# Attention scores: the last halving and the sum over four partitions done by TensorE into the softmax layout

## The chip, the core and the metric

The kernel runs on one core of one Trainium2 chip. The metric is the device time of one execution in microseconds (us). Engines are named as in the profile: PE is TensorE (matrix products; PEld its weight loads), DVE is VectorE, ACT is ScalarE, POOL is GpSimd, SP is SyncE, which issues most transfers. Each engine works through its own queue in order; an instruction that has to wait holds up everything behind it on that engine.

## What is computed

The input x has 2048 rows of 1024 in bf16. After a layer norm without weights it goes through two branches, and the output is x + s * g:

```
xn = layernorm(x)
qkv = xn @ wqkv            # 32 heads of 32; q, k, v
logits[h, s, w] = (q[h, s] . k[h, s - 2w]) * 32**-0.5,  w = 0..7   (-1e9 where s - 2w < 0)
s  = (softmax(logits, over w) . v[h, s - 2w]) @ wo
g  = silu( (silu(xn @ w1) * (xn @ w3)) @ w2 )          # w1, w3: 1024 x 3584, w2: 3584 x 1024
out = x + s * g
```

So each position attends to eight positions, two apart, in its own head.

## The kernel before

The rows are worked in two blocks (b) of 1024, each of two chunks (c) of 512 positions. Layer norm and a transpose on PE (`ln_tp`) give xT, features on partitions. `qkv(c)` makes q, k and v of a chunk with 3 x 8 groups of 8 matmuls; each group fills one of the eight PSUM banks, and ACT casts it to SBUF (L220): q into `qo`, k into `kT`, v into `vT`. `kT` and `vT` hold one chunk and a halo of 16 older positions, which POOL copies from the chunk before (L201, L202) ahead of the new casts. The MLP's products (`mlp_up` in 14 parts `fb`, `mlp_down`) are done with a Strassen-like scheme that trades matmuls for additions on DVE and copies on ACT. One part of `mlp_up` has the groups ua, ue, ub; its last group (with `a22` and `t4`, "the tail") is put off into the next part through `pend`, and `flush` emits it. `wo(c)` multiplies the attention's result by wo and DVE (L541, L542) applies gate and residual.

The feature dimension of q and k is laid out so that partition p of slice j holds feature 8p + j of the 1024, so a head's 32 features lie in 4 neighbouring partitions of all 8 slices. `attention(c)` therefore works in these steps:

- Scores, for each of the 8 offsets w: DVE multiplies q by the shifted kT in two halves of four slices (L236, 128x2048 each), adds the halves (L238), halves again (L239) and once more (L240) into `E[:, w]`. What is left is a sum over 4 neighbouring partitions.
- Softmax layout: 16 transfers issued by POOL (L244) take every fourth partition of E into two tiles L, so that a partition is a head and a quarter of the positions; three DVE adds (L248 to L250) sum the four partitions into z, in fp32.
- Softmax on z: for chunk 0 a mask (L252), max tree, subtraction (L255), exp on ACT (L256), sum tree, reciprocal (L260), product into `pb` (L261). 16 transfers on POOL (L264) spread pb back over E, each value to the four partitions of its head.
- PV: DVE multiplies E by the shifted vT (L272) and adds up (L280, L286, L287) into `qo`.

`E` has one buffer. Intermediate tiles of the attention (`p_t`, `L`, `z`, `zm`, `zs`, `pb`, `B`, `C`) share a pool of three. A scheduling layer orders each engine's instructions when the program is built: by priority in the order in which the code emits them, filling in lower ones where it expects an engine to be free; `tc.high_priority()` moves instructions ahead. The emitted order is:

```
    for b in range(NB):
        qkv(c0); ...; mlp_up(b, range(cut[b])); attention(c0); flush(); qkv(c1)
        mlp_up(b, range(cut[b], FB)); flush(); attention(c1); mlp_down(b); wo(c0)
    wo(3)
```

with cut = (11, 10), FB = 14, and the wo of a block's second chunk behind the next block's first qkv. In block 0, DVE also makes sums of the weights in each part (`w_sums`, `w2_sums`, four adds each). At the start of `mlp_down`, DVE makes sums of h (L463, L464, L478, L490).

Of the kernel before, what the change touches and what calls it, by code (L numbers as in the profile page):

```python
# [9 lines left out]
BF16 = mybir.dt.bfloat16  # L10
FP16 = mybir.dt.float16
ACTF = mybir.ActivationFunctionType
ALU = mybir.AluOpType
# [4 lines left out]
def kernel(  # L18
# [21 lines left out]
    nc = tc.nc  # L40
    P = 128
    S, D, F = 2048, 1024, 3584
    Dh, W, DIL = 32, 8, 2
    KT = D // P
    KH = KT // 2
    CH = 512
# [6 lines left out]
    HALO = 16  # L53
    NJ = 8
    NR = 4
# [12 lines left out]
    const = ctx.enter_context(tc.tile_pool(name="const", bufs=1))  # L68
# [5 lines left out]
    att = ctx.enter_context(tc.tile_pool(name="att", bufs=3))  # L74
# [12 lines left out]
        out=ident[:], in_=ident[:], compare_op=ALU.not_equal, fill=1.0,  # L87
        base=0, pattern=[[-1, P]], channel_multiplier=1,
# [3 lines left out]
    nc.gpsimd.affine_select(  # L92
        out=maskb[0:32], in_=maskb[0:32], compare_op=ALU.is_ge, fill=-1.0e9,
        base=0, pattern=[[-DIL, W], [1, HALO]], channel_multiplier=0,
    )

    kT = keep.tile([P, NJ, HALO + CH], BF16, name="kT")
# [5 lines left out]
    E = keep.tile([P, W, CH], BF16, name="E")  # L103
# [21 lines left out]
    def bank(name):  # L125
        return psum.tile([P, CH], FP32, tag="mm", name=name)
# [97 lines left out]
    def tree(t, z, op):  # L224
        op(t[:], z[:, 0:4, :], z[:, 4:8, :])
        op(t[:, 0:2, :], t[:, 0:2, :], t[:, 2:4, :])
        op(t[:, 0:1, :], t[:, 0:1, :], t[:, 1:2, :])

    def attention(c):
        qT = qo[:, c % 2]  # L230
        for w in range(W):
            o = HALO - DIL * w
            pr = []
            for jh in range(2):
                p_t = att.tile([P, 4, CH], BF16, tag="a4")
                nc.vector.tensor_mul(p_t[:], qT[:, jh * 4:jh * 4 + 4, :], kT[:, jh * 4:jh * 4 + 4, o:o + CH])  # L236
                pr.append(p_t)
            nc.vector.tensor_add(pr[0][:], pr[0][:], pr[1][:])  # L238
            nc.vector.tensor_add(pr[0][:, 0:2, :], pr[0][:, 0:2, :], pr[0][:, 2:4, :])  # L239
            nc.vector.tensor_add(E[:, w, :], pr[0][:, 0, :], pr[0][:, 1, :])  # L240
        L = [att.tile([P, 2, W, P], BF16, tag="a4", name=f"L{c}_{i}") for i in range(2)]
        for r in range(NR):
            for sq in range(4):
                nc.gpsimd.dma_start(  # L244
                    out=L[r // 2][sq * 32:(sq + 1) * 32, r % 2, :, :], in_=E[r:P:NR, :, sq * P:(sq + 1) * P],
                )
        z = att.tile([P, W, P], FP32, tag="a4", name=f"z{c}")
        nc.vector.tensor_add(z[:], L[0][:, 0], L[0][:, 1])  # L248
        nc.vector.tensor_add(z[:], z[:], L[1][:, 0])
        nc.vector.tensor_add(z[:], z[:], L[1][:, 1])  # L250
        if c == 0:
            nc.vector.tensor_add(z[:, :, 0:HALO], z[:, :, 0:HALO], maskb[:])  # L252
        zm = att.tile([P, W // 2, P], FP32, tag="a4", name=f"zm{c}")
        tree(zm, z, nc.vector.tensor_max)
        nc.vector.tensor_sub(z[:], z[:], zm[:, 0:1, :].to_broadcast([P, W, P]))  # L255
        nc.scalar.activation(out=z[:], in_=z[:], func=ACTF.Exp, scale=scale)  # L256
        zs = att.tile([P, W // 2, P], FP32, tag="a4", name=f"zs{c}")
        tree(zs, z, nc.vector.tensor_add)
        pb = att.tile([P, W, P], BF16, tag="a4", name=f"pb{c}")
        nc.vector.reciprocal(out=zs[:, 0, :], in_=zs[:, 0, :])  # L260
        nc.vector.tensor_mul(pb[:], z[:], zs[:, 0:1, :].to_broadcast([P, W, P]))  # L261
        for r in range(NR):
            for sq in range(4):
                nc.gpsimd.dma_start(  # L264
                    out=E[r:P:NR, :, sq * P:(sq + 1) * P], in_=pb[sq * 32:(sq + 1) * 32, :, :],
                )
        for jh in range(2):
            js = slice(jh * 4, jh * 4 + 4)

            def pvmul(dst, w):  # L270
                o = HALO - DIL * w
                nc.vector.tensor_mul(  # L272
                    dst, E[:, w, :].unsqueeze(1).to_broadcast([P, 4, CH]), vT[:, js, o:o + CH]
                )

            A = qT[:, js, :]
            pvmul(A, 0)
            B = att.tile([P, 4, CH], BF16, tag="a4")
            pvmul(B[:], 1)
            nc.vector.tensor_add(A, A, B[:])  # L280
            for w0 in (2, 4, 6):
                B = att.tile([P, 4, CH], BF16, tag="a4")
                C = att.tile([P, 4, CH], BF16, tag="a4")
                pvmul(B[:], w0)
                pvmul(C[:], w0 + 1)
                nc.vector.tensor_add(B[:], B[:], C[:])  # L286
                nc.vector.tensor_add(A, A, B[:])  # L287
# [259 lines left out]
    for b in range(NB):  # L547
        c0, c1 = 2 * b, 2 * b + 1
        qkv(c0, partial(ln_transpose, 1) if b == 0 else None)
        if b == 0:  # L550
            w2_load(0)
        else:
            wo(c0 - 1)
        xn_sums()
        mlp_up(b, range(cut[b]))
        attention(c0)
        flush()
        qkv(c1)
        mlp_up(b, range(cut[b], FB))
        flush()  # L560
        attention(c1)
        mlp_down(b)
        wo(c0)
# [31 lines left out]
```

## Time and profile before

| | us |
|---|---|
| time, median of 2 runs (768.35 and 770.64) | 769.5 |
| span of the profiled execution, first to last instruction | 766.9 |
| PE busy, 3516 matmuls | 749.4 |
| DVE busy, 828 instructions | 602.1 |
| ACT busy, 534 instructions | 321.1 |
| POOL busy, 172 instructions | 97.2 |
| score multiplies L236, 64 of 1.215 | 77.5 |
| last halving L240, 32 of 0.414 | 13.3 |
| transfers E to L, L244, 64 issues of 0.586 | 37.0 |
| additions of L, L248 to L250, 12 of 1.217 | 14.6 |
| transfers pb to E, L264, 64 issues of 0.582 | 36.8 |

The busy time of a group is the sum of its durations, in which neighbouring instructions can overlap: matmuls with 512 columns last 0.379 us each and follow each other faster than that. A row of the order in time has the start, the length, engine, line, operation, what it writes and reads, how many instructions are merged, and in brackets the engine's idle time just before with what ended it. The page's chain follows the work that ended last back from the last instruction.

### The profile page before, as it was taken

How to read it: one execution, taken by the hardware profiler on the slowest of the kernel's cores; microseconds unless marked ns; L12 is line 12 of the kernel's file. 1: busy time of each engine (PE TensorE's matmuls, PEld its weight loads, DVE VectorE, ACT ScalarE, POOL GpSimd, SP SyncE). 2: the span in 40 equal slices, each digit the busy share in tenths (PEclk: the TensorE clock that was granted, in tenths of full speed). 3: DMA queues.
4: the chain of work that ended last, by engine and by line, in shares of the span. 5: the costliest groups of instructions: out<-in, count | busy, mean ns of one | idle time of the engine just before them, and what ended most of it. 6: DMA issues, size and time to landing. Idle time of an engine off the chain costs nothing.

```text
span 766.9 us, 9404 instructions
## 1 busy us (share of the span) xinstructions
PE 749.4 (98%) x3516; PEld 375.6 (49%) x3516; DVE 602.1 (79%) x828; ACT 321.1 (42%) x534; POOL 97.2 (13%) x172
## 2 busy tenths in 40 slices
PE   7999999999899999999999899999999999999997
PEld 4664444444565444445566344444466544444443
DVE  6479988887998999150799998565995995924997
ACT  5536444654225489264033044464433444321200
POOL 0000042132000001413000004040000004040000
PEclk8999999999999999999999999999999999999999
DMA  9633799898753668658853836565535257464634
GB/s 331 217 111 108 234 302 272 275 285 297 261 189 83 218 227 268 172 190 262 261 179 103 270 114 169 175 195 165 187 115 201 98 172 207 157 196 147 200 100 140
DMA packets 123117, 150.56 MB, mean 196 GB/s; under 512 B 6080, under 2 KB 97728, under 8 KB 119488
## 3 DMA queue, kind: packets, MB, share of 16 engines
q1 hardware_dynamic: 110336, 115.36, 48.2%
q0 software_dynamic: 8128, 30.42, 11.7%
q10 hardware_dynamic: 4608, 4.20, 1.6%
q8 instruction: 27, 0.44, 0.3%
q14 instruction: 18, 0.15, 0.1%
HBM read 115.34 MB, written 26.21 MB: 185 GB/s over the span
## 4 chain that ended last, share of the span: by engine, by line
PE 86%; DVE 8%; DMA 4%; issue 1%; ACT 1%; SPq 0%; DVEq 0%; ACTq 0%
PE ub L120 18%; PE qkv L120 15%; PE ue L120 12%; PE ua L120 12%; PE db L120 9%; PE de L120 6%; PE da L120 6%; PE s L120 5%; DMA wt<-in_A_wqkv_dram 2%; DVE B L286 1%; DVE B L272 1%; DVE qo L287 1%; DVE p_t L236 1%; PE tp L182 1%; DVE C L272 1%
## 5 line engine op out<-in xcount | busy, mean ns | idle before, releaser
L120 PE MATMUL qkv<-xT,wt 128*128 128x512 bf16 x768 | 169.9, 383 | 4.9 <-DMA wt<-in_A_wqkv_dram 4.4
L120 PEld LDWEIGHTS <-wt 128*128 128x128 bf16 x768 | 110.1, 144 | 63.8 <-DMA wt<-in_A_wqkv_dram 5.8
L120 PEld LDWEIGHTS <-st 128*128 128x128 f16 x896 | 87.7, 98 | 107.4 <-issue 1.7
L120 PE MATMUL ua<-xT,w 128*128 128x512 bf16 x448 | 106.7, 381 | 2.9 <-ACT ub L131 2.9
L120 PEld LDWEIGHTS <-w 128*128 128x128 bf16 x672 | 65.9, 98 | 84.0 <-issue 5.9
L120 PE MATMUL ub<-xs,st 128*128 128x512 f16 x448 | 106.7, 381 | 0.0
L120 PEld LDWEIGHTS <-h_sb 128*128 128x128 bf16 (+1 forms) x672 | 65.5, 98 | 77.5 <-issue 0.5
L236 DVE TENSOR_TENSOR p_t<-qo,kT 128x2048 bf16<-128x2048 bf16 x64 | 77.5, 1215 | 8.5 <-ACT kT L220 8.5
L120 PE MATMUL db<-wt,h_sb 128*128 128x512 f16 x336 | 73.7, 379 | 0.0
L374 DVE TENSOR_TENSOR us<-ue,us 128x512 f32<-128x512 f32 x56 | 37.5, 685 | 38.3 <-PE ue L120 38.3
L120 PE MATMUL s<-wot,qo 128*128 128x512 bf16 x256 | 55.7, 379 | 0.0
L367 ACT ACTIVATE h_sb<-ua 128x512 bf16<-128x512 f32 x56 | 33.3, 598 | 53.3 <-PE ua L120 53.3
L385 ACT ACTIVATE sg<-us 128x512 bf16<-128x512 f32 x56 | 34.8, 630 | 46.7 <-DVE us L374 46.7
L120 PE MATMUL ub<-xs,w 128*128 128x512 f16 x224 | 53.4, 379 | 0.9 <-DVE h_sb L383 0.9
L120 PE MATMUL ue<-xs,st 128*128 128x512 f16 x224 | 52.9, 379 | 0.1
L120 PE MATMUL ue<-xT,st 128*128 128x512 bf16 x224 | 52.9, 379 | 0.0
L131 ACT COPY ub<-ua 128x512 f32<-128x512 f32 x56 | 31.6, 570 | 44.4 <-PE ua L120 25.4
L120 PE MATMUL da<-wt,h_sb 128*128 128x512 bf16 x224 | 49.2, 379 | 0.3 <-DMA wt<-in_B_w_dram 0.3
L264 POOL DMA_DIRECT2D E<-pb x64 | 36.8, 582 | 92.9 <-DVE pb L261 89.1
L397 DVE TENSOR_TENSOR h_sb<-h_sb,ub 128x512 bf16<-128x512 bf16 x56 | 37.0, 679 | 14.4 <-PE ub L120 14.4
L244 POOL DMA_DIRECT2D L<-E x64 | 37.0, 586 | 59.3 <-DVE E L240 55.6
L220 ACT CAST qo<-qkv 128x512 bf16<-128x512 f32 x32 | 18.6, 585 | 61.3 <-PE qkv L120 45.0
(103 smaller groups left out, 841.1 us busy)
## 6 DMA issues: line engine op xcount, KB each, us to landing
wt<-in_A_wqkv_dram SPq DMA_DIRECT2D x24, 1024.0 KB, 7.1
w<-in_B_w_dram SPq DMA_DIRECT2D x42, 512.0 KB, 5.1
s_dram<-st POOLq DMA_DIRECT2D x14, 1024.0 KB, 5.9
wt<-t_dram SPq DMA_DIRECT2D x16, 896.0 KB, 5.4
st<-s_dram SPq DMA_DIRECT2D x14, 1024.0 KB, 5.3
wt<-in_B_w_dram SPq DMA_DIRECT2D x12, 896.0 KB, 6.1
wot<-in_A_wo_dram SPq DMA_DIRECT2D x8, 1024.0 KB, 7.9
w2q<-in_B_w_dram SPq DMA_DIRECT2D x14, 512.0 KB, 3.8
```

The lines of the kernel that those rows point to most:

```text
L120: nc.tensor.matmul(ps[:], lhsT=lhs[k], rhs=rhs[k], start=(first and k == 0), stop=(k == n - 1), skip_group_check=not first,)
L131: nc.scalar.copy(out=dst[:], in_=src[:])
L182: nc.tensor.matmul(tp[:, k * P:(k + 1) * P], lhsT=xt4[:, st, kt * P:(kt + 1) * P], rhs=ident[:], start=(k == 0), stop=(k == KH - 1), skip_ ...
L220: nc.scalar.copy(out=dst, in_=ps[:])
L236: nc.vector.tensor_mul(p_t[:], qT[:, jh * 4:jh * 4 + 4, :], kT[:, jh * 4:jh * 4 + 4, o:o + CH])
L244: nc.gpsimd.dma_start(out=L[r // 2][sq * 32:(sq + 1) * 32, r % 2, :, :], in_=E[r:P:NR, :, sq * P:(sq + 1) * P],)
L264: nc.gpsimd.dma_start(out=E[r:P:NR, :, sq * P:(sq + 1) * P], in_=pb[sq * 32:(sq + 1) * 32, :, :],)
L272: nc.vector.tensor_mul(dst, E[:, w, :].unsqueeze(1).to_broadcast([P, 4, CH]), vT[:, js, o:o + CH])
L367: nc.scalar.activation(out=h_sb[:, fl[i], 0:CH], in_=pa[i][:], func=ACTF.Silu)
L374: m = nc.vector.tensor_add(su2[i][:], pe[i][:], su2[i][:])
L385: nc.scalar.activation(out=sg2[i][:], in_=su2[i][:], func=ACTF.Silu)
L397: nc.vector.tensor_mul(h_sb[:, fl[i], 0:CH], h_sb[:, fl[i], 0:CH], pb[i][:])
```

## The change

The last halving and the sum over four partitions are done by PE. `bones` is a 128x32 matrix of ones and zeros with bones[p, h] = 1 where p // 4 = h, built once by POOL. E now holds, for four offsets at a time, the two slices that are left after L239's halving (`E4`, 4 offsets x 2 slices x 512 positions). For each half of the offsets, eight matmuls with `bones` as the weights sum over the four partitions and the two slices, and write heads and quarters of positions straight into the layout of z in one PSUM bank, `zb`; ACT copies the bank into z.

```diff
+    bones = const.tile([P, 32], BF16, name="bones")
+    nc.gpsimd.memset(bones[:], 1.0)
+    nc.gpsimd.affine_select(
+        out=bones[:], in_=bones[:], compare_op=ALU.is_ge, fill=0.0,
+        base=0, pattern=[[-NR, 32]], channel_multiplier=1,
+    )
+    nc.gpsimd.affine_select(
+        out=bones[:], in_=bones[:], compare_op=ALU.is_ge, fill=0.0,
+        base=NR - 1, pattern=[[NR, 32]], channel_multiplier=-1,
+    )
...
     def attention(c):
         qT = qo[:, c % 2]
-        for w in range(W):
-            o = HALO - DIL * w
-            pr = []
-            for jh in range(2):
-                p_t = att.tile([P, 4, CH], BF16, tag="a4")
-                nc.vector.tensor_mul(p_t[:], qT[:, jh * 4:jh * 4 + 4, :], kT[:, jh * 4:jh * 4 + 4, o:o + CH])
-                pr.append(p_t)
-            nc.vector.tensor_add(pr[0][:], pr[0][:], pr[1][:])
-            nc.vector.tensor_add(pr[0][:, 0:2, :], pr[0][:, 0:2, :], pr[0][:, 2:4, :])
-            nc.vector.tensor_add(E[:, w, :], pr[0][:, 0, :], pr[0][:, 1, :])
-        L = [att.tile([P, 2, W, P], BF16, tag="a4", name=f"L{c}_{i}") for i in range(2)]
-        for r in range(NR):
-            for sq in range(4):
-                nc.gpsimd.dma_start(
-                    out=L[r // 2][sq * 32:(sq + 1) * 32, r % 2, :, :], in_=E[r:P:NR, :, sq * P:(sq + 1) * P],
-                )
+        E4 = E[:].rearrange("p (w j) t -> p w j t", j=2)
         z = att.tile([P, W, P], FP32, tag="a4", name=f"z{c}")
-        nc.vector.tensor_add(z[:], L[0][:, 0], L[0][:, 1])
-        nc.vector.tensor_add(z[:], z[:], L[1][:, 0])
-        nc.vector.tensor_add(z[:], z[:], L[1][:, 1])
+        for wh in range(2):
+            for w4 in range(4):
+                o = HALO - DIL * (wh * 4 + w4)
+                pr = []
+                for jh in range(2):
+                    p_t = att.tile([P, 4, CH], BF16, tag="a4")
+                    nc.vector.tensor_mul(p_t[:], qT[:, jh * 4:jh * 4 + 4, :], kT[:, jh * 4:jh * 4 + 4, o:o + CH])
+                    pr.append(p_t)
+                nc.vector.tensor_add(pr[0][:], pr[0][:], pr[1][:])
+                nc.vector.tensor_add(E4[:, w4], pr[0][:, 0:2, :], pr[0][:, 2:4, :])
+            zb = bank(f"zb{c}_{wh}")
+            for jj in range(2):
+                for sq in range(4):
+                    nc.tensor.matmul(
+                        zb[sq * 32:(sq + 1) * 32, :], lhsT=bones[:], rhs=E4[:, :, jj, sq * P:(sq + 1) * P],
+                        start=(jj == 0), stop=(jj == 1), skip_group_check=True,
+                    )
+            with tc.high_priority():
+                nc.scalar.copy(out=z[:, wh * 4:wh * 4 + 4, :], in_=zb[:].rearrange("p (w t) -> p w t", w=4))
```

Below, line numbers of the kernel before are used for instructions that both kernels have.

## The prediction

> **What bounds the kernel now.** I read the page's busy shares and chain first, then who waited for whom on TensorE (PE), then the order in time of PE, VectorE (DVE) and GpSimd (POOL) around the four attention calls. Busy shares, then the chain's shares by engine:
>
> ```profile
> PE 749.4 (98%) x3516; PEld 375.6 (49%) x3516; DVE 602.1 (79%) x828; ACT 321.1 (42%) x534; POOL 97.2 (13%) x172
> ...
> PE 86%; DVE 8%; DMA 4%; issue 1%; ACT 1%; SPq 0%; DVEq 0%; ACTq 0%
> ```
>
> PE is the bound; DVE is idle for 165 us of the span. PE's own waits (us in total, times, longest):
>
> ```profile
> PE qkv L120 <- DMA wt<-in_A_wqkv_dram: 4.4, 3, 3.5
> PE ua L120 <- ACT ub L131: 2.9, 1, 2.9
> PE ub L120 <- DVE h_sb L383: 0.9, 3, 0.4
> ```
>
> No row has PE waiting for attention: scores, softmax and PV run on DVE, POOL and ScalarE (ACT) beside the MLP's matmuls. PE in order of time (start, length, work, idle before):
>
> ```profile
> 186.85 1.89 PE L120 MATMUL ub<-xs,st 128*128 128x512 f16 x8
> 189.07 1.89 PE L120 MATMUL ub<-xs,w 128*128 128x512 f16 x8 [0.33 <-DVE h_sb L383]
> 194.50 5.79 PE L120 MATMUL qkv<-xT,wt 128*128 128x512 bf16 x18 [3.55 <-DMA wt<-in_A_wqkv_dram]
> ...
> 350.92 0.83 PE L182 MATMUL tp<-ident,x 128*128 128x128 bf16 x12
> 351.59 0.38 PE L120 MATMUL db<-wt,h_sb 128*128 128x512 f16 x1
> ...
> 379.00 41.60 PE L120 MATMUL qkv<-xT,wt 128*128 128x512 bf16 x192
> ...
> 440.79 2.76 PE L120 MATMUL ua<-xT,w 128*128 128x512 bf16 x8 [2.92 <-ACT ub L131]
> 443.34 2.75 PE L120 MATMUL ub<-xs,st 128*128 128x512 f16 x8
> 445.93 1.89 PE L120 MATMUL ue<-xT,st 128*128 128x512 bf16 x8
> ```
>
> Start to start, a 512-column matmul takes 41.6/192 = 0.216 us and a 128-column one (351.59 - 350.92)/12 = 0.056. After an idle of 2.9 us the next two groups of 8 take 2.55 and 2.59 us where others take 1.73: a restart costs 1.7 us, and the granted clock there is 0.71. DVE in order of time, then POOL:
>
> ```profile
> 194.91 1.22 DVE L272 TENSOR_TENSOR qo<-E,vT 128x2048 bf16<-128x2048 bf16 x1
> ...
> 225.94 1.22 DVE L272 TENSOR_TENSOR C<-E,vT 128x2048 bf16<-128x2048 bf16 x1
> ...
> 230.70 2.35 DVE L236 TENSOR_TENSOR p_t<-qo,kT 128x2048 bf16<-128x2048 bf16 x2
> 232.97 1.22 DVE L238 TENSOR_TENSOR p_t<-p_t 128x2048 bf16<-128x2048 bf16 x1
> 234.22 0.69 DVE L239 TENSOR_TENSOR p_t<-p_t 128x1024 bf16<-128x1024 bf16 x1
> 234.83 1.22 DVE L236 TENSOR_TENSOR p_t<-qo,kT 128x2048 bf16<-128x2048 bf16 x1
> ...
> 673.71 1.23 DVE L261 TENSOR_TENSOR pb<-z,zs 128x1024 bf16<-128x1024 f32 x1
> ...
> 692.13 1.23 DVE L272 TENSOR_TENSOR qo<-E,vT 128x2048 bf16<-128x2048 bf16 x1 [16.19 <-DMA E<-pb]
> ```
>
> ```profile
> 227.32 1.12 POOL L202 COPY vT<-vT 128x128 bf16<-128x128 bf16 x1 [31.48 <-DVE C L272]
> ...
> 342.08 9.15 POOL L264 DMA_DIRECT2D E<-pb x16 [26.82 <-DVE pb L261]
> ```
>
> **Removed.** Per chunk: 8 adds of L240 (0.34 us start to start), 3 z additions (1.14) and 16 L transfers (9.3 us of POOL issue). All of it lies beside PE: worth 0 on the path, 24 us of DVE in sum. It could pay only where PE waits for a late DVE. That is the 2.92 us at 440.79: the forks (L131) waited 18.9 us in all for DVE's o_t of L541 to free banks, and DVE was late there with chunk 1's PV. With PV done earlier (below) I take that wait and its restart away: -4.6 (ends 0 and -4.6).
>
> **Moved onto PE's queue.** The changed kernel's instructions stand thus. Scores are made in two halves of four offsets. zb's first 8 matmuls stand just before the last s4 group ("tail") of the MLP part ahead of the attention, the second 8 right behind it (chunks 1 and 3: 1 ahead of the last tail group, 15 behind), and all qkv or `da` matmuls behind those. DVE cannot begin the second half's E before the first 8 matmuls have read E, which has one buffer. So PE now waits at the second 8 until DVE has made a half. A half: two multiplies 2.27 us, add 1.25, E add 0.61, and 0.12 where the add follows its own multiply (as 1.25 against 1.14 above): 4.25 per offset, 17.0 in all. From the tail's end to E ready:
>
> - Chunk 0: DVE has the last L397 (0.8 with the signal), two w_sums (1.2), four w2_sums (1.34) and the half, 16.8 as its first steps are interleaved: 20.1. The weights' wait of 3.55 and two later ones (0.84) fall inside: 20.1 - 3.55 - 0.84 = +15.7. The restart was paid before.
> - Chunk 1: L397 0.8, eight L463/L464 at 1.0, one w2_sum and small steps 1.3, the half 17.0: 27.1; restart 1.7; two small waits (0.4) gone: +28.4.
> - Chunk 2: 0.8 and the half less one multiply already done, 15.8: 16.6; restart 1.7, an old 0.41 gone: +17.9.
> - Chunk 3: half of the L463/L464 lie ahead of the tail's end: 0.8 + 0.6 + 4.0 + 3.2 + 17.0 = 25.6; restart 1.7: +27.3.
>
> **What is late next.** In chunks 0 and 2 everything from the softmax to PV now starts with qkv of the next chunk, where it was over or begun before. From the end of zb: copy 0.8, mask 0.3 (chunk 0), max and subtract 2.7, table and exp 2.4, sums to pb 3.7, transfers, PV to its last C 32.25 (194.91 to 227.16), vT's halo copy 1.3, first vT cast 0.8. For the transfers there are two rows: pb's end 674.94 to 692.13 is 17.2; 9.15 of issue and the page's median landing of 4.6 give 14.1 after pb; I take the middle, 15.6. Sum 59.9 (chunk 2: 59.6). PE has 192 matmuls ahead of it, 41.6 + 1.7 = 43.3, and then needs a PSUM bank that holds v, as all 8 do. It waits 16.6 and 16.3 more, with a second restart each: +18.3 and +18.0. In chunks 1 and 3 the same chain has `mlp_down` (89 us, 276 to 365) as cover: 0; without it up to 60.
>
> **Added.** 64 matmuls with 512 columns moving and 32 output columns. 14 lie inside the waits; 50 count. No row has 32-column weights. By moving columns 0.216 each, 10.8; a quarter of the array writes as much as a 128-column matmul, so 0.056, 2.8. They are as near to one row as to the other: middle, 6.8, both ends kept. The 8 z copies on ACT (0.57, as L131) are in the chain above; `bones` costs POOL three short steps at the start, 0.8 by the rows of `ident` and `maskb` (0.2 + 0.3 + 0.3), with 185 us until its first use.
>
> The Trainium skill bears on this price. "TensorE: Matmul & The Clock Gate", Part 3 (packing small matmuls), says matmuls that write different 32-row slices of PSUM run at once; an estimate by it is a quarter of 10.8, and the time would be 4 us below mine. Against the change, "TensorEngine Tiling (Array Packing)", Key Properties, says a change of tiling mode drains TensorE; with 0.38 - 0.22 = 0.16 us left after the last start and 16 changes, an estimate is +2.6. No run here shows either.
>
> **Sum.** 15.7 + 28.4 + 17.9 + 27.3 = 89.3 first waits; 18.3 + 18.0 = 36.3 second waits; 6.8 matmuls; -4.6. Together +127.8 on the profiled execution's span of 766.9: 894.7. The median 769.5 lies 2.6 above that span, for the work around it: **897 us**.
>
> **Rivals.**
> 1. DVE runs ahead and E is ready when PE comes: no first waits, then PV as early as before. For it: DVE's 165 idle us, 24 more freed. Against it: the second half's writes wait for zb's first half, which stands 1.7 us ahead of the second. It decides if that order lets DVE start 17 us sooner. Then +6.8 - 4.6: 772, not slower. Chance 0.03.
> 2. The second waits are hidden: qkv's v banks are cast late but nothing needs them. It decides if PV ends within 43 us of zb, a chain shorter by 17. For it: in the trace vT's halo copy held ACT up only by 6.9 us in all. Against: the terms are rows, and the 32.25 of PV alone leaves 11. 897 - 36 = 861. Chance 0.09.
> 3. DVE backlog: after the second wait DVE owes chunk 1's (3's) first half beside the MLP. Three (four) MLP parts at 12.1 us of PE and some 8 to 9 us of DVE leave 3 to 4 each; if nothing of it is left, up to 17 us show in each: 897 + 34 = 931. Against: at 246 to 275 DVE had as much and PE waited 0.2. Chance 0.09.
> 4. The four matmuls that write the four partition slices of zb run at once: 50 x 0.216/4 = 2.7, so 893. No row shows two matmuls at once; chance 0.35, inside the forecast's own range. (The Trainium skill's rule above says it would be so.)
>
> That the change doesn't do what it says I leave out: the instructions named as removed are gone from the queues.
>
> **Numbers.** Forecast 0.44 and rival 4 0.35 share a range: zb 2.8 to 10.8 and 2.6 of drains (-4 to +6.6), transfers 14.1 to 17.2 twice (-3 to +3.2), the 4.6 not gained (+4.6): 890 to 912. Out to rivals 2 and 3: 861 to 931; each of these has a spread of its own, so that about 0.15 with rival 1 is left out. Faster by over 2% 0.01, within 2% 0.02, slower by over 2% 0.97; 2% is about what a measurement of this kernel tells from no change.
>
> **What would show it.** Four waits of PE in `zb` rows on DVE E, 17 to 27 us long, just behind the last `ub` tails; two waits of `ua` on ACT vT of about 17 us behind qkv of chunks 1 and 3; the granted clock near 0.7 behind each; no wait of `ua` near wo(1). PE's busy time up by 3 to 11 us, DVE's down by 24 to 28. Wrong would be: E written before the tail; vT cast on time; zb groups of 8 taking far from 0.45 to 1.7 us at full clock; waits of PE inside the MLP.

## The result and the profile after

| | before | after |
|---|---|---|
| time, median of 2 runs, us | 769.5 | 898.6 |
| span of the profiled execution | 766.9 | 896.2 |
| PE busy | 749.4 | 762.2 |
| PE not busy (span less busy) | 17.5 | 134.0 |

The kernel after is slower: the ratio is 1.166, with a 95% interval of 1.156 to 1.175. Forecast were 897 us and a rise of 127.8 in the span; the span rose by 129.3. Of this, 116.5 is time in which PE stands and 12.8 is time in which it works. From here on, lines of the kernel after and of the experiments are lines of those kernels: in the kernel after, L250 to L253 are the scores, L257 is zb, L284 PV and L231 the casts of q, k and v.

Busy shares and the chain's shares by engine, on the page of the kernel after:

```profile
PE 762.2 (85%) x3519; PEld 377.8 (42%) x3580; DVE 590.7 (66%) x784; ACT 322.1 (36%) x539; POOL 60.9 (7%) x111
...
PE 72%; DVE 21%; POOL 2%; DMA 2%; issue 2%; ACT 1%; SPq 0%; DVEq 0%; POOLq 0%; ACTq 0%
```

DVE has less to do than before (590.7 for 602.1 us), yet its share of the chain has gone from 8% to 21%: it is not busier, PE now stands for it. The rows of PE's waits (us in total, times, longest) say where:

```profile
PE zb L257 <- DVE E L253: 89.2, 4, 26.5
PE ua L131 <- ACT vT L231: 30.5, 2, 16.0
PE qkv L131 <- DMA wt<-in_A_wqkv_dram: 1.3, 2, 1.0
...
PE ua L131 <- ACT ub L142: 0.7, 1, 0.7
```

The first two rows are new and come to 119.7; the others were 4.4 and 2.9. PE in order of time shows where each wait stands and what follows it:

```profile
189.06 0.61 PE L257 MATMUL zb<-E,bones 128*32 128x512 bf16 x8
189.60 1.90 PE L131 MATMUL ub<-xs,w 128*128 128x512 f16 x8
211.83 1.05 PE L257 MATMUL zb<-E,bones 128*32 128x512 bf16 x8 [20.33 <-DVE E L253]
212.81 20.55 PE L131 MATMUL qkv<-xT,wt 128*128 128x512 bf16 x81
...
273.10 3.21 PE L131 MATMUL ua<-xT,w 128*128 128x512 bf16 x8 [14.47 <-ACT vT L231]
...
338.39 1.05 PE L257 MATMUL zb<-E,bones 128*32 128x512 bf16 x8 [26.50 <-DVE E L253]
...
639.55 1.04 PE L257 MATMUL zb<-E,bones 128*32 128x512 bf16 x8 [17.22 <-DVE E L253]
...
700.12 3.57 PE L131 MATMUL ua<-xT,w 128*128 128x512 bf16 x8 [16.04 <-ACT vT L231]
...
777.62 1.04 PE L257 MATMUL zb<-E,bones 128*32 128x512 bf16 x8 [25.11 <-DVE E L253]
```

Each chunk has one wait at the second zb group, behind the first and the 1.9 us of the tail; chunks 0 and 2 have a second wait one qkv later. A zb group itself takes 0.54 us from its start to the next one's, and 0.98 behind a wait.

### The profile page after: what moved, and what is told of

Same layout as the page of the kernel before. It is cut to its first block, busy times and chain, and to the rows that moved or that the text cites. A ratio compares the mean times of both kernels' runs of the same rounds, so it can differ in the third digit from the quotient of the medians.

```text
span 896.2 us, 9343 instructions
## 1 busy us (share of the span) xinstructions
PE 762.2 (85%) x3519; PEld 377.8 (42%) x3580; DVE 590.7 (66%) x784; ACT 322.1 (36%) x539; POOL 60.9 (7%) x111
## 4 chain that ended last, share of the span: by engine, by line
PE 72%; DVE 21%; POOL 2%; DMA 2%; issue 2%; ACT 1%; SPq 0%; DVEq 0%; POOLq 0%; ACTq 0%
PE ub L131 15%; PE ua L131 11%; PE ue L131 11%; PE qkv L131 10%; PE db L131 8%; PE s L131 6%; PE da L131 6%; DVE p_t L250 4%; PE de L131 4%; DVE B L284 2%; DVE p_t L252 2%; POOL E L276 2%; DVE C L284 2%; DVE qo L299 2%; DVE B L298 2%
## 5 line engine op out<-in xcount | busy, mean ns | idle before, releaser
L131 PE MATMUL qkv<-xT,wt 128*128 128x512 bf16 x751 | 172.1, 389 | 3.0 <-DMA wt<-in_A_wqkv_dram 1.3
L131 PE MATMUL ua<-xT,w 128*128 128x512 bf16 x441 | 108.5, 387 | 31.6 <-ACT vT L231 30.5
L250 DVE TENSOR_TENSOR p_t<-qo,kT 128x2048 bf16<-128x2048 bf16 x64 | 76.2, 1217 | 20.8 <-ACT kT L231 20.8
L257 PE MATMUL zb<-E,bones 128*32 128x512 bf16 x64 | 7.4, 502 | 89.2 <-DVE E L253 89.2
L409 DVE TENSOR_TENSOR h_sb<-h_sb,ub 128x512 bf16<-128x512 bf16 x56 | 37.1, 682 | 32.9 <-PE ub L131 32.9
L131 PE MATMUL da<-wt,h_sb 128*128 128x512 bf16 x218 | 51.5, 396 | 0.7 <-issue 0.4
L553 DVE TENSOR_TENSOR o_t<-s,xs 128x512 f32<-128x512 f32 x32 | 21.9, 688 | 35.3 <-PE s L131 35.3
```

Source lines behind the costliest of these rows:

```text
L131: nc.tensor.matmul(ps[:], lhsT=lhs[k], rhs=rhs[k], start=(first and k == 0), stop=(k == n - 1), skip_group_check=not first,)
L409: nc.vector.tensor_mul(h_sb[:, fl[i], 0:CH], h_sb[:, fl[i], 0:CH], pb[i][:])
L553: nc.vector.tensor_mul(o_t[:], ps[:], gt[:, dh * NST + st])
```

## The experiments

Four theories were tried. **T**, the forecast's: the time goes into PE standing in its queue for a half of the scores that is late, and after that for late PV. **M**: it goes into the zb matmuls themselves, some 16 us per group. **D**: DVE has too little time for the scores, whatever the order. And within T, what makes the half late: only E (**Te**), or E and a place in a pool (**Tp**). The kernels below were measured in three groups of four, each beside the kernel before, whose medians there were 770.4 (own_E, early, late, both), 771.8 (touch_z, own_E_touch_z, early_pv, both_pv) and 770.3 (warm, sq_outer, zb_x4, own_all). As these and the 769.5 above differ by up to 2.3, a difference of 2 us between kernels of two groups means little.

### own_E: E is not shared

Each offset has its own place in E, at the price of the third halving on DVE:

```diff
-                nc.vector.tensor_add(E4[:, w4], pr[0][:, 0:2, :], pr[0][:, 2:4, :])
+                nc.vector.tensor_add(pr[0][:, 0:2, :], pr[0][:, 0:2, :], pr[0][:, 2:4, :])
+                nc.vector.tensor_add(E[:, wh * 4 + w4, :], pr[0][:, 0, :], pr[0][:, 1, :])
...
-            for jj in range(2):
-                for sq in range(4):
+            for sq in range(4):
...
-                        zb[sq * 32:(sq + 1) * 32, :], lhsT=bones[:], rhs=E4[:, :, jj, sq * P:(sq + 1) * P],
-                        start=(jj == 0), stop=(jj == 1), skip_group_check=True,
+                    zb[sq * 32:(sq + 1) * 32, :], lhsT=bones[:], rhs=E[:, wh * 4:wh * 4 + 4, sq * P:(sq + 1) * P],
+                    start=True, stop=True, skip_group_check=True,
...
```

> The third halving is kept on DVE, so each offset has its own place in E, the second half of the scores no longer waits for the first zb group, and a zb group has 4 matmuls. Theory T (the loss is PE standing in its queue at the second zb group for a half of the scores that could not begin before the first group had read E, and after that late PV): the waits of zb on DVE vanish in chunks 0, 2 and 3, where DVE had time ahead of the tail (it was free of scores from 722 to 752 in chunk 3), the wqkv weights' wait of 3.5 comes back, chunk 1 still waits 25 to 29, since DVE was busy 37.8 of 39 us ahead of it, and both vT waits stay at 13 to 16: 898.6 - 16.4 - 16.8 - 25 - three restarts of 2.5 + 2 for the adds = about 835 (828 to 845). Rival M (the zb matmuls or their mode cost the time, some 16 us per group of 8): half the matmuls, so about 834 too, but with PE's time in matmuls and not in waits. Rival D (DVE has too little time for the scores, whatever the order): waits stay within 3 us of what they were, 890 to 905.

Measured: 902.7 us, ratio 1.172 (1.169 to 1.175). The theory missed by 68. Not one wait has gone; its row of PE's waits:

```profile
PE zb L256 <- DVE E L253: 97.1, 4, 28.4
```

DVE of the same run, in order of time around chunk 0:

```profile
61.16 0.42 DVE L253 TENSOR_TENSOR E<-p_t 128x512 bf16<-128x512 bf16 x1
65.11 0.69 DVE L385 TENSOR_TENSOR us<-ue,us 128x512 f32<-128x512 f32 x1 [3.53 <-PE ue L131]
...
193.25 1.22 DVE L249 TENSOR_TENSOR p_t<-qo,kT 128x2048 bf16<-128x2048 bf16 x1
```

The fourth offset is done at 61.6. DVE then stands for 3.5 us for PE and makes no scores until 193, though q, k and E are there: the products of the fifth offset are not waiting for anything, they stand far behind in DVE's queue. The kernel after shows the same in chunk 3, where DVE had little else to do:

```profile
722.38 0.69 DVE L253 TENSOR_TENSOR E<-p_t 128x1024 bf16<-128x1024 bf16 x1
...
760.40 2.35 DVE L250 TENSOR_TENSOR p_t<-qo,kT 128x2048 bf16<-128x2048 bf16 x2
```

The products write `p_t`, not E, so E cannot be what kept them. M is half refuted as well: half the matmuls in as many groups, the same time. D fits the number, and so does a second hold.

### touch_z and own_E_touch_z: the place in the pool

What the products need is a buffer of the pool of three, and in the code `z` stands ahead of them but is written for the first time when ACT copies the first zb group. If z holds the place of the second half's buffers until then, an earlier write to z frees them. The edit is one line, on the kernel after and on own_E:

```diff
         z = att.tile([P, W, P], FP32, tag="a4", name=f"z{c}")
+        nc.gpsimd.memset(z[:, 0, 0:1], 0.0)
```

> The kernel after, and POOL writes one column of z ahead of the scores of each chunk, so that z takes its place in the pool of three (a4) before the scores do and not at its first copy from zb; E is still shared by both halves. Theory Tp (two things hold the second half: its first products need p_t buffers, which come behind z in the pool, and z is taken only when the first zb group has run; and its sums need E): DVE can make one pair of products and their sum ahead, 3.5 us, and no more, so the four zb waits fall by 2.5 to 3.5 each (89.2 to about 77) and the time is about 886 (880 to 892). Theory Te (only E holds it): no change, 896 to 901. Rival D (DVE has too little time): no change.

> own_E with the same early write of z, so that neither E nor the pool holds the second half. Tp: the zb waits of chunks 0 and 2 vanish and the weights' wait of 3.5 comes back; chunk 3 keeps 8 to 10 (the sums of h and the last offset behind the tail); chunk 1 keeps 25 to 29, as DVE is busy in the three parts ahead of it; both vT waits stay at 13 to 16, since softmax and PV still begin with the next qkv: 898.6 - 16.3 - 16.8 - 16 - restarts 5 = about 845 (835 to 855). Te and D: as own_E, 898 to 906.

| | E shared | E not shared |
|---|---|---|
| z first written by the copy | 898.6 (after) | 902.7 (own_E) |
| z written early | 880.9 (touch_z) | 852.8 (own_E_touch_z) |

touch_z: ratio 1.143 (1.140 to 1.147); the four zb waits are 15.5, 24.6, 12.4 and 20.4, 73.0 in all for 89.2. Three of them fell by 4.7 to 4.8 and not by 3.5, as DVE also makes one product of the next pair. own_E_touch_z: ratio 1.107 (1.103 to 1.111), with these waits:

```profile
PE zb L257 <- DVE E L254: 39.6, 3, 28.4
PE ua L131 <- ACT vT L231: 33.1, 2, 16.7
PE qkv L131 <- DMA wt<-in_A_wqkv_dram: 4.5, 3, 3.1
PE ua L131 <- ACT ub L142: 3.0, 1, 3.0
```

So there are two holds in series. Freeing E alone gains nothing, freeing the pool alone 17.7, both 45.9. With both free the waits of chunks 0 and 2 are gone or nearly so (39.6 is 28.4 of chunk 1, 10.9 of chunk 3 and 0.3), the weights' wait of 3.1 is back, and the vT waits are as they were. That one early write frees the products shows that z's place is the second hold; how the building hands out the places is not to be seen in a trace. Te falls and D falls, but for chunk 1: there DVE was busy 37.8 of the 39 us ahead of the tail in the kernel after, and the 28.4 stays.

### early and early_pv: the first chunk's attention stands earlier

`attention` is taken apart into scores and zb of one half, softmax (`soft`) and PV (`pv`), which are emitted behind parts of `mlp_up`. In `early`, PV goes along with the softmax; in `early_pv` it stays behind the last part:

```diff
-        mlp_up(b, range(cut[b]))
-        attention(c0)
+        mlp_up(b, range(cut[b]), {1: [partial(scores, c0, 0)], 5: [partial(scores, c0, 1), partial(soft, c0)]})
+        pv(c0)
```

> For the first chunk of each block the first zb group stands behind part 1 of the MLP and the second, with softmax and PV, behind part 5, in place of part 10 (9); the second chunk of each block stands as it did. Theory T: both waits of chunks 0 and 2 vanish, zb on DVE (20.3 and 17.2) and ua on vT (14.5 and 16.0), with their restarts (some 8 in all); the weights' waits of 4 to 5 come back; chunks 1 and 3 still wait 25 to 28: 898.6 - 68 + 5 - 8 = about 827 (820 to 836). M: 64 matmuls as before, so 895 to 902. D: the waits return inside the MLP parts or in chunks 1 and 3, 850 or more.

Measured: 859.9, ratio 1.117 (1.114 to 1.119). The two vT waits and the zb waits of chunks 0 and 2 are gone, and 51.6 of zb is left for chunks 1 and 3, as expected. But there is a new wait of 31.3, and the time is 33 above the 827 expected; by the time alone it lies in D's range (850 or more). PE's rows:

```profile
PE zb L261 <- DVE E L257: 51.6, 2, 26.5
PE ue L131 <- DVE st L354: 31.8, 2, 31.3
```

DVE at the end of that wait:

```profile
212.34 1.22 DVE L306 TENSOR_TENSOR B<-B,C 128x2048 bf16<-128x2048 bf16 x1
213.47 0.68 DVE L354 TENSOR_TENSOR st<-w 128x1024 f16<-128x1024 bf16 x1
214.07 1.22 DVE L307 TENSOR_TENSOR qo<-qo,B 128x2048 bf16<-128x2048 bf16 x1
```

The weight sums (`st`) of the next part have PV's B and qo rows directly ahead of them: PV, emitted earlier, had come before them in DVE's queue. This is the same fault as in the change itself, made by the experiment: the engine that bounds stands for work put ahead of what it needs.

> As the run early (zb of the first chunk of each block behind parts 1 and 5, softmax behind part 5), but PV emitted at its old place behind part 10 (9), so that it does not stand ahead of the next part's weight sums on DVE, for which PE stood 31.3 us in early. Theory T (PE loses time only where it stands for DVE in its queue): the waits of chunks 0 and 2 vanish, chunks 1 and 3 keep 26.5 and 25.1: 859.9 - 31.3 - 2 to 3 for the restart = about 826 (820 to 832). Rival: the DVE work only moves, and another wait of 10 or more appears in the MLP: 836 to 860.

Measured: 832.3, ratio 1.080 (1.077 to 1.084), just above the theory's range: the 31.3 is gone, no other long wait has come in the MLP, and the weights' waits are 8.3 where the expectation of `early` had 4 to 5. So the wait in `early` was PV's place in the queue, and not DVE having too little time (D).

### late, both, both_pv and own_all: the second chunk too

The second zb group, softmax and PV of the second chunk of each block stand inside `mlp_down` (in `late` and `both` behind the T2 products; in `both_pv` so in block 0, and behind the first gate products in block 1). The cut is that of `both_pv`; in the other two, softmax and PV are one function:

```diff
-        attention(c1)
-        mlp_down(b)
+        scores(c1, 0)
+        mlp_down(b, (partial(scores, c1, 1), partial(soft, c1), partial(pv, c1)))
```

> For the second chunk of each block the second zb group, softmax and PV stand 36 us further on, behind the T2 products of mlp_down; the first chunk of each block stands as it did. Theory T: the zb waits of chunks 1 and 3 (26.5 and 25.1) and their restarts (about 2 each) vanish, the four waits of chunks 0 and 2 stay: 898.6 - 51.6 - 4.5 = about 842 (836 to 852, the upper end if PV is late for wo(3)). M: 895 to 902. D: 870 or more.

> Both moves together, with all 64 zb matmuls. Theory T: no wait on scores or vT is left, the sum of the two gains: 898.6 - 71 - 56 = about 771 (766 to 780), the time before plus 3 to 4 us of zb matmuls on PE and with the weights' waits back, and the wait at the first ua of block 1 gone or back (-4.6 or 0). M: 895 to 902. D: 800 or more, with waits of zb or of ua on DVE in the MLP.

> early_pv, and in the second chunk of each block the second zb group, softmax and PV stand inside mlp_down: behind the T2 products in block 0 (36 us on), behind the first gate products in block 1 (24 us on, since PV was 10.0 us late for the last wo in the run both). Theory T: no wait on scores is left but up to 5 us of zb in block 1: 771 to 780, within 2% of the time before (770.4), though all 64 zb matmuls are done. M (the matmuls themselves cost): 820 or more.

`late` took 856.3 (ratio 1.112, 1.110 to 1.115): the zb waits of chunks 1 and 3 are gone (37.5 is left, chunks 0 and 2), and the last `wo` stands 10.0 us for PV, so it is 4 above the range. `both` took 820.7 (1.066, 1.063 to 1.069), far over the 780 expected and by the time alone in D's range (800 or more); its long waits are the 31.3 of `early` and the 10.0 of `late`, and none is on scores. `both_pv` took 788.2 (1.023, 1.019 to 1.027), 8 above the range; its waits:

```profile
PE qkv L131 <- DMA wt<-in_A_wqkv_dram: 6.8, 4, 4.6
PE s L131 <- DVE qo L310: 6.3, 1, 6.3
...
PE zb L261 <- DVE E L257: 1.1, 1, 1.1
```

All 64 zb matmuls are there, and of the 129 us some 16 are left: M is refuted. What is left is mostly PV late for the last `wo` and weights that come later, not scores.

The last of this line, `own_all`, keeps the third halving on DVE, emits all scores ahead of z, and has both zb groups together where E is sure to be ready:

```diff
+    def zsum(c):
+        zt[c] = att.tile([P, W, P], FP32, tag="a4", name=f"z{c}")
...
+        mlp_up(b, range(cut[b]), {1: [partial(scores, c0, 0), partial(scores, c0, 1)], 6: [partial(zsum, c0), partial(soft, c0)]})
+        pv(c0)
...
+        mlp_down(b, (partial(zsum, c1), partial(soft, c1), partial(pv, c1)))
```

> The third halving is kept on DVE, E holds all eight offsets, all scores are emitted ahead of z, and both zb groups (4 matmuls each) stand where E is sure to be ready: behind part 6 in the first chunk of each block, 36 us into mlp_down in block 0, 12 us into it in block 1; softmax behind them, PV of the first chunks at its old place. Theory: nothing of the loss is left but the matmuls, and the wait of wo for PV (6.3 in both_pv) goes as PV of the last chunk starts 12 us earlier: 788.2 - 6.3 - 2 - 2 = about 778 (773 to 784), still not under the time before (771), since PE is the bound and has 32 matmuls more. Rival: DVE, which has the third halving back, is late in block 0 or 1: 784 to 800.

Measured: 784.1, ratio 1.017 (1.014 to 1.020): at the edge of the theory's range and in that of the rival, and both are partly right. No wait for scores or PV is left, but

```profile
PE qkv L131 <- DMA wt<-in_A_wqkv_dram: 9.6, 4, 5.3
PE ub L131 <- DVE h_sb L414: 3.3, 4, 1.7
PE ue L131 <- DVE st L360: 2.9, 1, 2.9
PE ua L131 <- ACT ub L142: 2.4, 1, 2.4
```

come to 18.2, where the kernel before had 8.2 in the three rows that the prediction shows. PE is busy for 751.7 us, 2.3 more than before. So the change can be had for about 14 us in place of 129. `own_all` is within 2% of the kernel before, but its interval lies above 1, and so do those of all the others; no version tried beats the kernel before: PE had no wait on the scores there that could be saved.

### warm: does PE's standing slow what follows?

On the kernel after; the extra matmuls write into the bank that zb then overwrites:

```diff
             zb = bank(f"zb{c}_{wh}")
+            if wh == 1:
+                flush()
+                for i in range((90, 118, 75, 111)[c]):
+                    m = nc.tensor.matmul(zb[:], lhsT=ident[:], rhs=kT[:, 0, 0:CH], start=True, stop=True, skip_group_check=True)
...
```

> The kernel after, and PE is given 90, 118, 75 and 111 matmuls of 128 columns of weights and 512 moving columns between the last tail group and the second zb group of chunks 0 to 3, work that fits just inside the waits there (19.4, 25.5, 16.2 and 24.0 of 20.3, 26.5, 17.2 and 25.1 us); their result is overwritten by the zb group. The waits of ua on vT are not filled. If what follows a long wait is slow because the clock granted to PE has sunk (0.50 for some 4 us and 0.64 to 0.88 for 4 more in the kernel after), the granted clock stays at 1.00 there and 2 to 3 us per chunk are saved, 898.6 - 9.5 = about 889 (886 to 892). By the 1.7 us of the forecast: 892 to 894. If the slow start has nothing to do with PE standing idle: 897 to 900.

Measured: 890.5, ratio 1.156 (1.153 to 1.159), 8.1 less than the kernel after, though PE has some 390 matmuls more. PE in order of time around the first wait of `warm`:

```profile
191.54 19.59 PE L258 MATMUL zb<-kT,ident 128*128 128x512 bf16 x88
212.15 0.61 PE L263 MATMUL zb<-E,bones 128*32 128x512 bf16 x8 [1.03 <-DVE E L253]
212.70 18.14 PE L131 MATMUL qkv<-xT,wt 128*128 128x512 bf16 x81
```

The same 81 qkv matmuls take 18.14 for 20.55. The granted clock is the third number from the end of each row here; first the kernel after behind that wait, then `warm`:

```profile
212.00:216.00 4.00, 4.00 (x16) 1.38 (x9) 2.26 (x5) 0.59 (x1) 0.00 (x0) 0.50 0.00 0
216.00:220.00 4.00, 3.85 (x15) 2.11 (x14) 1.19 (x2) 3.40 (x4) 0.00 (x0) 0.78 0.01 2
```

```profile
213.00:217.00 4.00, 4.00 (x20) 2.70 (x19) 2.93 (x5) 1.41 (x3) 0.00 (x0) 1.00 0.00 0
```

In chunk 0, then, qkv and the zb group run 2.4 + 0.4 us faster. A mean of 0.78 over 4 us is 1.8 at half clock, so PE ran at half clock until 217.8, for 5.9 us from the end of the wait. The same reckoning behind all six waits of the kernel after; at half clock half of the time is lost, which is an estimate that agrees with the 2.8 of chunk 0:

| wait | ends at | clock in two rows of 4 us from there | us at half clock | lost |
|---|---|---|---|---|
| zb, chunk 0 | 211.8 | 0.50, 0.78 | 5.9 | 3.0 |
| zb, chunk 1 | 338.4 | 0.50, 0.74 | 5.7 | 2.8 |
| zb, chunk 2 | 639.6 | 0.50, 0.94 | 4.9 | 2.5 |
| zb, chunk 3 | 777.6 | 0.63, 1.00 | 3.4 | 1.7 |
| vT, chunk 0 | 273.1 | 0.65, 1.00 | 2.7 | 1.4 |
| vT, chunk 2 | 700.1 | 0.50, 0.76 | 5.8 | 2.9 |

Behind the zb waits that is 10.0 in all, and the whole kernel gained less. In chunk 2 the vT wait grew from 16.0 to 17.9 and took up most of what qkv had gained; and behind the vT wait of chunk 0, which was not filled, the clock stayed at half for 5.6 us in `warm` and for 2.7 in the kernel after. The 8.1 is uncertain too: `sq_outer` below, measured beside `warm` and with the same waits as the kernel after, is only 6.0 above it. The Trainium skill ("TensorE: Matmul & The Clock Gate", Part 1) has the clock go up after at least one busy window of some 3.4 us, and the windows run freely; by an estimate 1.7 or more is lost. Five of the six losses here are 1.7 to 3.0, and one, with 1.4, is below it.

### sq_outer and zb_x4: the price of a zb matmul

`sq_outer` exchanges the two loops on the kernel after; `zb_x4` runs each group four times over on `both_pv`:

```diff
-            for jj in range(2):
-                for sq in range(4):
+            for sq in range(4):
+                for jj in range(2):
...
-            for jj in range(2):
+            for jj in [0, 1] * 4:
```

> The kernel after, with the two loops around the zb matmuls exchanged: the two matmuls that add up into the same 32 partitions of zb follow each other, and matmuls into different partitions are neighbours only at each second step. If the four groups of 32 columns run at once (rival 4), a pair must run one after the other and a group of 8 takes about 5 x 0.216 = 1.1 us in place of 0.54 at full clock, twice that behind a wait: 4 x 0.54 + 4 x 1.1 = 6.5 more, 905 (902 to 908). If each matmul costs a fixed 0.068 us for its small size: no change, 897 to 900.

> both_pv with each zb group run four times over (the same sums, written again), 192 more matmuls at full clock. Four at once: 8 x 3 x 0.54 = 13.0 more than 788.2, 801 (797 to 805). By the middle that the forecast took (0.135 each): 814. One after the other at 0.216: 41 more, 829.

`sq_outer` took 896.5 (1.164, 1.162 to 1.167), half a microsecond under the range of no change, and a group of 8 the same 0.55:

```profile
187.20 1.89 PE L131 MATMUL ub<-xs,st 128*128 128x512 f16 x8
189.02 0.62 PE L257 MATMUL zb<-E,bones 128*32 128x512 bf16 x8
189.57 1.90 PE L131 MATMUL ub<-xs,w 128*128 128x512 f16 x8
```

`zb_x4` took 798.6 (1.037, 1.035 to 1.040), 10.4 more than `both_pv` for 192 matmuls, 0.054 each (PE's busy time rose by as much, from 753.3 to 763.7); its row has 32 of them in 1.85:

```profile
79.67 1.91 PE L261 MATMUL zb<-E,bones 128*32 128x512 bf16 x32
81.52 1.90 PE L131 MATMUL ua<-xT,w 128*128 128x512 bf16 x7
```

So a 128x32 matmul with 512 columns moving costs 0.058 to 0.068, between a quarter and a third of the 0.216 of a full one. A picture in which the two sums into one slice must follow each other and block the queue is refuted. Whether four matmuls run at once from queues of their own, or each is short, these runs do not tell. The Trainium skill ("TensorEngine Tiling (Array Packing)", Key Properties) says tiles work independently, with which the same time in both orders agrees, though it does not show it. The drain that the page names at a change of mode does not show with the forecast's 0.16: the zb group at 189.02 starts 0.09 later than 187.20 and 8 x 0.216 would have it, and with 0.55 it takes 0.09 more than 8 x 0.058, so that two changes cost at most 0.18 where the forecast allowed 0.32.

## Why the prediction was right, and where it was not

- **The first waits** were forecast at 20.1, 27.1, 16.6 and 25.6 and came at 20.3, 26.5, 17.2 and 25.1. The place and the sum of DVE's rows were right. The cause given was half of it: "DVE cannot begin the second half's E before the first 8 matmuls have read E, which has one buffer" is true (touch_z), but the products, which do not touch E, were late as well, behind z's place in the pool (own_E). The sum came out because it took the whole half as late, which one E buffer alone would not give: with E the only hold, touch_z, the waits are 16 us shorter in all.
- **The second waits**, forecast at 16.6 and 16.3, were 14.5 and 16.0. From the end of zb to the first ua the chain took 273.10 - 212.81 = 60.3 (59.9 forecast), and the transfers from pb to PV 15.7 (15.6). PE's 192 matmuls ahead took 45.8 and not 43.3, as the slow clock and two weights' waits of 1.3 fell into them. `early_pv` shows that both waits go when softmax stands earlier.
- **The zb matmuls**, 6.8, were taken too dear: 50 x 0.068 = 3.4. Rival 4's 2.7 and the forecast's lower end, 2.8, were nearer; which of their reasons holds, four at once or short matmuls, is not settled.
- **The restarts** were too cheap: 1.7 each behind three zb waits and two vT waits, 8.5. By the granted clock these five lost 11.3 (2.8, 2.5 and 1.7; 1.4 and 2.9). Chunk 0, taken as paid before, lost 3.0, where the kernel before had lost some 1.7 (its clock was 0.50 from 195.9 to 199.3). The granted clock, forecast near 0.7, was 0.50 to 0.65 in the first 4 us. That the restarts and the zb matmuls miss in opposite ways and by much the same is luck, and so in part is a time that is right within 2 us.
- **The wait near wo(1)**, 2.92, fell to 0.71, as the -4.6 assumed. It was 3.0 and 2.4 again in own_E_touch_z and own_all, so the reason given (PV earlier) is not enough; it was not followed further.
- **Idle and busy.** The forecast's terms hold 114.2 of waits (89.4 + 32.9 less 5.2 of DMA waits and 2.9) and 13.6 of work; measured 116.5 and 12.8. The page's signs were missed: PE's busy time was to rise by 3 to 11 and rose by 12.8, as slow matmuls count as busy; DVE's was to fall by 24 to 28 and fell by 11.4. The durations of DVE's groups, added up, did fall by 25.1 (646.5 to 621.4), but neighbours overlap, and in the kernel after they do so for less of the time (30.7 for 44.4).
- **Rivals.** 1 (DVE ahead of PE) fell with four waits in the row of zb; 2 (second waits hidden) with the 30.5; 3 (backlog in the MLP) as no row of waits shows PE standing there for scores or sums.

## What to carry to other kernels

A small step moved onto the engine that bounds costs its place in that queue, not its time: here 3 to 4 us of matmuls brought 120 us of waits, because they were put where their input could not be ready, and nearly all of it went when they were put 36 us later or some parts earlier. Before blaming a shared buffer, list everything that the late producer needs, the order in which a pool hands out buffers too: with two holds in series, freeing one can show nothing, as in own_E. And work emitted earlier to be ready sooner must not come to stand ahead of what the bound engine needs next on the same queue, as PV did in `early`.

## What was not expected of the hardware

- A matmul with 32 columns of weights and 512 moving columns costs 0.058 us in runs of 32 and 0.068 in runs of 8; in runs of 8 the order of its output slices made no difference.
- Behind six waits of PE of 14 to 27 us the granted clock was 0.50 for 2.7 to 5.9 us, and 1.00 after that. The length does not follow that of the wait: 3.4 us behind 25.1, 4.9 behind 17.2, 5.9 behind 20.3. With the four zb waits filled with matmuls, the whole kernel was 6 to 8 us faster.
